# One core, sparse attention followed by a max-out layer: the written-out order of all tasks, the engines of the copies and the buffers exchanged for another set

## The chip, the cores and the metric

The kernel runs on one core of one Trainium2 chip. The metric is the device time of one execution in microseconds, lower is better. The core has a matrix engine (TensorE, PE in the profile, with its weight loads shown apart as PEld), VectorE (DVE), ScalarE (ACT), GpSimd (POOL), and SyncE (SP), which here only issues transfers. Each engine works through its own list of instructions in order and waits at semaphores for the others. Transfers run on 16 DMA engines beside them.

## The reference, cut to what matters

Four batches, eight heads, 768 positions, 64 values a head. Each query sees the 15 keys on either side of it and itself, and beside them 24 block keys: for every block of 32 keys their maximum, with the mean of the block's values.

```
k_sum = k.reshape(B, H, nb, 32, D).max(axis=3)
v_sum = v.reshape(B, H, nb, 32, D).mean(axis=3)
scores_l = scale * q @ k.T            # kept where |i - j| < 16
scores_s = scale * q @ k_sum.T + log(32)
a = softmax(concat(scores_l, scores_s))
x = (a @ concat(v, v_sum)).transpose(0, 2, 1, 3).reshape(3072, 512)
out = maximum(x @ w1, x @ w2) @ w_out     # w1, w2: 512 x 1024; w_out: 1024 x 512
```

Inputs and output are float32; the kernel computes in bfloat16 with float32 sums.

## The kernel before, in words

**Tasks.** The kernel first describes its whole work as 780 tasks (`op`, from line 140 of the listing on). A task is a small piece for one engine: one load, one cast of a loaded tile, three transposes, the score matrices of four windows, one exponential, one quarter of a hidden layer. It names the buffers it reads and writes. A buffer belongs to a `Ring`, a small set of slots of one tile shape (13 `land` tiles for loads, 8 PSUM banks, 4 `kqb`, 2 `vx`, 10 output tiles `o`, of which six lie in tiles that held w1 before, shown as `w1t` and `w1b`). A slot is given to the next buffer when the earlier one's last reader is done, and if a task is placed earlier than that, its engine waits.

**What sets the order.** `Plan.run` can find an order by replaying the tasks with assumed durations, but this kernel does not run it. It carries the outcome as three tables: `CFG["order"]`, the numbers of the tasks in the order in which they are issued; `CFG["engines"]`, a letter a task, which tells of a task that can run on several engines the one that it gets (T PE, D DVE, A ACT, P POOL, S a transfer by SP); and `CFG["slots"]`, the slot that each new buffer takes. `given` (line 225) emits the tasks by these tables:

```
    def given(self, order, slots):
        for t in order:
            for b in self.tasks[t].new:
                if b.slot is None:
                    b.take(slots.pop(0))
            self.tasks[t].fn(self.tasks[t].letter)
```

Since every engine keeps to its list, the tables fix what stands behind what on each engine and in SP's queue of transfers.

**Stages.** Batch 0 comes first: `prep` casts k and q (L596 and L598 are the copy helper: casts, placements, copies), turns them by TensorE (L629, into PSUM) and places them; the block maxima are L655. `spread_v` prepares v: copies shifted by half a window into `vx`, block means by TensorE (L523, L569) and their copies into `vx` (from `apart` in batch 0, from `sums` later). `scores` is L706 (its mask in batch 0 is a matmul, L695, later a product on DVE, L730), the exponential is L720 on ACT, `values` L762 and L767, the division L818 and L821 on DVE into `xs`. `xs` is turned into `xt`, by TensorE in batch 0 (L836 and a copy) and by a DMA transpose from SP in the later batches (L827). Some of k and q of batches 2 and 3 are also turned by DMA transposes (L633). Early in the kernel, TensorE has nothing real to do for stretches, and 14 pairs of matmuls on the identity (L990, `warm`) stand there.

**Weights.** `load_w12` loads w1 and w2 in four quarters of two pieces each (L857). `wd n` (L865) is the difference w2 - w1 of quarter n in bfloat16: one instruction on DVE or four on POOL. The max-out is computed as relu(x (w2 - w1)) and x w1, the latter folded into w1 w_out (`w1o`, L905). `maxout` multiplies by `wd` (L921, "hidden", eight matmuls of 256 columns; hidden quarters 1 and 3 in the task names need wd 1 and wd 3, the others wd 0 and wd 2), takes the relu (L930 on ACT, L932 on DVE), and `out_part` adds x w1o (L948) and g w_out (L955), copies the bank to an `o` tile (L598) and stores it (L966, L968) from SP's or ACT's queue.

A task name such as "hidden 023" means batch 0, group of positions 2, quarter 3; "scores 321" batch 3, heads 4 to 7, group 1; "copy out 121" batch 1, group 2, half 1.

## Time and profile before

| | |
|---|---|
| median of 3 runs | 165.75 us (164.71 to 165.79) |
| the profiled execution's own time | 165.96 us |
| its span, first to last instruction | 164.2 us |
| TensorE busy | 153.8 us, 94% of the span |
| weight loads, DVE, ACT, POOL busy | 100.0, 112.1, 92.9, 63.6 us |
| matmuls | 1812 |
| read from and written to HBM | 25.17 MB, 6.29 MB |

An execution's time is its span and some 1.8 us around it. Busy times are unions, so pipelined instructions are not counted twice. The clock that was granted to TensorE is 1.00 in every stretch.

### The profile page before, as it was taken

Reading aid. Unit: us, or ns where it says so; the run is one execution under the profiler, and the core shown is the slowest. Engines: PE = TensorE matmul, PEld = TensorE weight load, DVE = VectorE, ACT = ScalarE, POOL = GpSimd, SP = SyncE. Lnnn points to the kernel's source line nnn. Section 1 sums busy time; section 2 is a strip of 40 time slices with the busy share of each in tenths; the row PEclk is TensorE's granted clock in tenths of the full one; section 3 lists DMA queues with packets and bytes.
Section 4 is the critical chain, followed back from the end, with each engine's and each line's share of the span. In section 5 each row is a group of like instructions: output and inputs, shape, how many; then the busy total and the mean of one; then the engine's idle time right before and its main releaser. Section 6 shows DMA issues by size and latency. Waiting matters only on the chain.

```text
span 164.2 us, 4482 instructions
## 1 busy us (share of the span) xinstructions
PE 153.8 (94%) x1812; PEld 100.0 (61%) x1812; DVE 112.1 (68%) x224; ACT 92.9 (57%) x134; POOL 63.6 (39%) x123
## 2 busy tenths in 40 slices
PE   5789977999999999999999999999899999999992
PEld 2346656998465554676687646778545467766651
DVE  3697797579866799977979974759756655063221
ACT  3469986694677698938796645382927312012010
POOL 6059949403343389654673654034730000000000
PEclk9999999999999999999999999999999999999999
DMA  4999999999999899997989996897999987111015
GB/s 155 288 326 309 254 364 371 395 379 381 288 191 271 176 290 258 157 260 131 205 187 241 226 151 106 208 268 144 239 230 360 305 156 187 36 64 70 0 67 188
DMA packets 67700, 36.46 MB, mean 222 GB/s; under 512 B 54624, under 2 KB 61664, under 8 KB 67680
## 3 DMA queue, kind: packets, MB, share of 16 engines
q1 hardware_dynamic: 66208, 33.76, 86.1%
q10 hardware_dynamic: 1472, 2.43, 4.4%
q8 instruction: 14, 0.23, 0.6%
q14 instruction: 6, 0.05, 0.1%
HBM read 25.17 MB, written 6.29 MB: 192 GB/s over the span
## 4 chain that ended last, share of the span: by engine, by line
PE 74%; DVE 9%; DMA 8%; SPq 2%; issue 2%; ACT 2%; ACTq 0%; DVEq 0%
PE banks L955 22%; PE banks L921 19%; PE banks L948 11%; DMA out_dram<-o 6%; PE banks L905 4%; PE banks L629 4%; PE banks L762 4%; PE banks L706 3%; DMA land<-in_k_dram 2%; PE banks L990 2%; DVE vx L598 2%; SPq L827 2%; DVE ks L655 2%; DVE kx L598 1%; DVE xs L821 1%
## 5 line engine op out<-in xcount | busy, mean ns | idle before, releaser
L955 PE MATMUL banks<-wo,g 128*128 128x512 bf16 (+2 forms) x208 | 46.5, 363 | 0.0
L921 PE MATMUL banks<-xt,wd 128*128 128x256 bf16 x384 | 45.5, 273 | 0.0
L921 PEld LDWEIGHTS <-wd 128*128 128x128 bf16 x384 | 37.3, 98 | 7.3
L955 PEld LDWEIGHTS <-g 128*128 128x128 bf16 x208 | 18.7, 98 | 17.3
L720 ACT ACTIVATE pb<-banks 128x1024 bf16<-128x1024 f32 x24 | 23.6, 1026 | 7.8 <-PE banks L706 5.4
L948 PE MATMUL banks<-w1o,xt 128*128 128x512 bf16 (+2 forms) x104 | 23.7, 363 | 0.3 <-DVE o L598 0.3
L932 DVE TENSOR_SCALAR g<-banks 128x512 bf16<-128x512 f32 x21 | 14.1, 685 | 8.7 <-PE banks L921 8.5
L930 ACT ACTIVATE g<-banks 128x512 bf16<-128x512 f32 x27 | 15.2, 603 | 8.1 <-PE banks L921 8.0
L598 POOL COPY vx<-sums 32x792 bf16<-32x792 bf16 x15 | 14.8, 988 | 12.6 <-ACT sums L598 7.1
L730 DVE TENSOR_TENSOR pb<-pb,mask 128x1024 bf16<-128x1024 bf16 (+1 forms) x24 | 16.1, 697 | 4.2 <-ACT pb L720 3.8
L821 DVE TENSOR_TENSOR xs<-banks,inv 128x512 bf16<-128x512 f32 x24 | 16.0, 687 | 3.6 <-DMA xt<-xs 3.0
L598 ACT COPY o<-banks 128x512 f32<-128x512 f32 (+1 forms) x8 | 4.4, 545 | 24.8 <-PE banks L955 23.7
L596 POOL CAST kqb<-land 128x256 bf16<-128x256 f32 (+1 forms) x22 | 10.9, 528 | 18.7 <-DMA land<-in_q_dram 9.8
L948 PEld LDWEIGHTS <-xt 128*128 128x128 bf16 x104 | 9.9, 98 | 9.7 <-issue 0.5
L655 DVE TENSOR_REDUCE ks<-kx 128x24 bf16<-128x768 bf16 x16 | 15.0, 944 | 0.2
L596 POOL CAST vx<-land 128x384 bf16<-128x384 f32 x20 | 10.6, 554 | 8.3 <-DMA land<-in_v_dram 8.3
L598 DVE COPY o<-banks 128x512 f32<-128x512 f32 (+2 forms) x10 | 6.2, 620 | 10.9 <-PE banks L955 8.8
L598 DVE CAST kqb<-land 128x768 bf16<-128x768 f32 x12 | 7.2, 612 | 6.7 <-DMA land<-in_k_dram 2.7
L629 PE MATMUL banks<-ident,kqb 128*128 128x128 f32 x60 | 9.6, 277 | 1.7 <-DVE kqb L598 1.7
L598 ACT CAST kqb<-land 128x768 bf16<-128x768 f32 x11 | 10.4, 944 | 1.2 <-DMA land<-in_k_dram 1.1
L762 PEld LDWEIGHTS <-pb 128*64 128x64 bf16 (+1 forms) x384 | 7.9, 110 | 4.7 <-issue 2.6
L762 PE MATMUL banks<-vx,pb 128*64 128x65 bf16 (+1 forms) x384 | 9.4, 196 | 1.2 <-DVE xs L821 0.6
(88 smaller groups left out, 183.4 us busy)
## 6 DMA issues: line engine op xcount, KB each, us to landing
land<-in_k_dram SPq DMA_DIRECT2D x16, 384.0 KB, 5.4
land<-in_v_dram SPq DMA_DIRECT2D x16, 384.0 KB, 6.8
land<-in_q_dram SPq DMA_DIRECT2D x16, 384.0 KB, 5.9
land<-in_moe_w_dram SPq DMA_DIRECT2D x8, 512.0 KB, 9.5
land<-in_moe_w_out_dram SPq DMA_DIRECT2D x4, 512.0 KB, 9.9
out_dram<-o SPq DMA_DIRECT2D x7, 256.0 KB, 2.3
out_dram<-o ACTq DMA_DIRECT2D x4, 256.0 KB, 3.2
out_dram<-w1t SPq DMA_DIRECT2D x3, 256.0 KB, 4.0
```

The costliest lines, as they stand in the source:

```text
L596: nc.gpsimd.tensor_copy(out=o[:, at:at + step], in_=i[:, at:at + step])
L598: {"D": nc.vector.tensor_copy, "A": nc.scalar.copy, "P": nc.gpsimd.tensor_copy}[e](out=o, in_=i)
L629: nc.tensor.transpose(out=bank(ps)[:, 128 * j:128 * j + 128], in_=src.ap[:].bitcast(F32)[:, 128 * j:128 * j + 128], identity=ident32[:])
L655: op("D", 0.95, lambda e: nc.vector.tensor_reduce(out=ks.ap[:, 0:nb], in_=free(kt(), 128, [256, NM], [192, 2], [32, 2], [1, 32]), axis=AX. ...
L720: op("A", {"A": 1.03}, lambda e: nc.scalar.activation(out=spread(pb.ap[:, 0, 0:1], [192, 8], [128, 2], [1, 64]) if PW > 128 else spread(pb ...
L730: nc.vector.tensor_tensor(out=o, in0=o, in1=spread(mask[:, 2 * u:2 * u + 1, 0:1], [0, n], [64, 2], [1, 64]), op=ALU.mult)
L762: nc.tensor.matmul(out=o, lhsT=p[r], rhs=vx[b].ap[r, par, hp + n, 2 * grp + u, a, 0:D + 1], start=(PW == 128 or par == 0), stop=(last and ...
L821: op("D", 0.69, lambda e: nc.vector.tensor_tensor(out=x.ap[:].rearrange("p n u a d -> p n (u a) d"), in0=spread(bank_tile[:, ps.ap, 0:1], ...
L921: nc.tensor.matmul(out=bank(ps)[:, 256 * s:256 * s + 256], lhsT=wd_tile[:, quarter, c, 128 * s:128 * s + 128], rhs=x.ap[:, c, :], start=(c ...
L930: nc.scalar.activation(out=o, in_=bank(ps), func=ACT.Relu)
L948: nc.tensor.matmul(out=bank(ps, c1 - c0), lhsT=x.ap[:, c, sl], rhs=w1o[c].ap[:, cols], start=(c == 0), stop=False)
L955: nc.tensor.matmul(out=bank(ps, c1 - c0), lhsT=g.ap[:, f, sl], rhs=wo[f // 2].ap[:, f % 2, cols], start=False, stop=(f == FC - 1))
```

## The change

The three tables are replaced; the tasks, their functions, their shapes and their dependencies stay as they are. 181 of the 780 tasks get another engine; the order is another one on every engine, and so are the slots. The DVE has 210 tasks before and after, ACT 143 before and 155 after, POOL 82 and 68, SP 106 and 108, TensorE 239 both times. The new tables were found by a replay in which VectorE may get in between the parts into which a GpSimd copy or difference is cut.

```
 CFG["order"] = list(map(int, """
-44 32 2 0 3 10 12 1 4 6 11 15 13 8 112 20 30 26 56 25 46 113 116 9 122 7 123 126 14 47 16 117 34 118 132 168 28 23 133
...
+4 32 3 26 30 31 19 112 113 27 1 0 2 44 116 10 12 15 16 46 56 132 122 9 117 123 25 133 34 6 118 11 13 33 126 14 128 119
...
 CFG["engines"] = "".join("""
-PDPPPDDDPAPDPDDDDPTTTTTTTTTTTTTTSSSAAAATDDPPSSSADPATAAPPSSSPDDPTADDDSSSPDDPTADDPSSDPTASSPATDSSDATDSSPATASDSASASDDTDTAD
...
+PPPDDDPDPAPPDPDDDPTTTTTTTTTTTTTTSSSAAAATADDDSSSPPDDTDADPSSSPPPPTADPPSSSDDDPTADDDSSDATASSPATASSPATASSPDTDSPSASDSPATATDD
...
 CFG["slots"] = list(map(int, """
-0 1 0 0 0 0 0 0 0 0 0 0 1 0 2 1 3 0 0 0 1 1 1 0 0 0 0 0 4 0 0 2 4 0 0 0 1 5 2 0 0 0 0 0 2 0 0 1 4 1 0 1 4 1 0 0 0 0 0
...
+0 0 1 0 1 0 0 1 1 0 0 0 0 0 2 3 0 1 0 0 0 1 0 0 4 0 0 0 0 5 1 0 0 0 0 1 0 0 2 4 2 0 0 0 0 0 1 0 0 1 0 2 1 0 1 6 7 2 0
...
```

Three places of the resulting lists follow. First DVE's list at the start of the kernel, where the first k tiles are prepared. `kqb` is a cast k or q tile, `kx` a placed one, `ks` its block maxima; `hide`, `amean`, `apart` are constants that are filled once. Before:

```order
L368 MEMSET apart_99 128x264
L390 COPY hide<-hide 64x64
L412 MEMSET amean 128x384
L393 COPY hide<-hide 128x128
L598 CAST kqb_75<-land_63 128x2x3x2x64
L598 CAST kqb_76<-land_62 128x2x3x2x64
L362 MEMSET apart_98 32x8x2
L362 MEMSET apart_99 32x8x2
L396 MEMSET hide 64x16
L397 MEMSET hide 32x48
L402 MEMSET amean 32x6x2 x4
L655 TENSOR_REDUCE ks_100<-kx_79 128x24
```

After:

```order
L337 MEMSET vx_95 128x96x2
L337 MEMSET vx_94 128x96x2
L598 COPY kx_79<-banks 128x6x2x64
L390 COPY hide<-hide 64x64
L412 MEMSET amean 128x384
L402 MEMSET amean 32x6x2 x4
L598 CAST kqb_75<-land_65 128x2x3x2x64
L655 TENSOR_REDUCE ks_100<-kx_79 128x24
L598 COPY kx_79<-kx_79 128x32
L396 MEMSET hide 64x16
L397 MEMSET hide 32x48
L598 COPY kx_79<-ks_100 128x6x2x32
```

The casts of the first two k tiles have gone to ACT, DVE places the first one, and the fillings of `hide` and `amean`, which stood ahead of anything loaded, now stand behind that placement.

Second, POOL's list around the differences of the weights (`wd`). Before:

```order
L596 CAST vx_94<-land_69 128x6x64 x2
L598 COPY vx_94<-vx_94 32x2x64
L596 CAST vx_94<-land_70 128x6x64 x2
L598 COPY vx_94<-vx_94 32x2x64
L598 COPY vx_94<-apart_99 32x528
L865 TENSOR_TENSOR wd<-land_62,land_65 128x256 x4
L865 TENSOR_TENSOR wd<-land_64,land_63 128x256 x4
L596 CAST w1b_124<-land_68 128x512 x2
```

After:

```order
L598 COPY vx_94<-vx_94 64x12x64
L598 COPY vx_94<-vx_94 32x2x64
L598 COPY vx_94<-apart_99 32x528
L598 COPY vx_94<-apart_98 32x528
L865 TENSOR_TENSOR wd<-land_62,land_64 128x256 x4
L865 TENSOR_TENSOR wd<-land_66,land_63 128x256 x4
L865 TENSOR_TENSOR wd<-land_69,land_68 128x256 x4
L596 CAST wo_130<-land_65 128x512 x2
```

The first two differences (wd 3 and wd 1) stay here; a third (wd 2), which DVE made before, is now behind them, and DVE keeps wd 0 alone. In SP's list the two pieces of wd 3 and of wd 1 are the 13th to 16th load in both kernels, behind twelve loads of q, k and v of batch 0; behind them come one k tile and then, after the change, the two pieces for wd 2 and the two for wd 0, where before a k tile stood among these four and the two of a pair were apart.

Third, SP's queue at the first store of the output (`out_dram<-o`, batch 0, group 0, half 0, "store 000") among the transposes of batch 2 (`xt`) and of k and q of batch 3 (`kt`). Before:

```order
L827 DMA_TRANSPOSE xt_113<-xs_110 128x4x128
L633 DMA_TRANSPOSE kt_104<-kqb_75 128x6x128
L428 DMA land_62<-in_k_dram 128x2x384
L827 DMA_TRANSPOSE xt_114<-xs_111 128x4x128
L827 DMA_TRANSPOSE xt_114<-xs_112 128x4x128
L428 DMA land_63<-in_q_dram 128x12x64
L966 DMA out_dram<-o_126 128x512
L827 DMA_TRANSPOSE xt_115<-xs_110 128x4x128
```

After:

```order
L428 DMA land_62<-in_q_dram 128x12x64
L470 DMA land_67<-in_v_dram 128x12x64
L966 DMA out_dram<-o_127 128x512
L827 DMA_TRANSPOSE xt_113<-xs_109 128x4x128
L633 DMA_TRANSPOSE kt_103<-kqb_75 128x6x128
L827 DMA_TRANSPOSE xt_113<-xs_110 128x4x128
L633 DMA_TRANSPOSE kt_104<-kqb_77 128x6x128
L827 DMA_TRANSPOSE xt_114<-xs_111 128x4x128
```

The store stands ahead of all transposes of batch 2, eight transfers earlier. In both kernels the copy "copy out 121" takes the `o` tile that this store empties. The second copy of that kind, "copy out 211", takes the tile that "store 011" empties; that store was the third of a run of three (111, 101, 011) and is the second now (111, 011).

## What the change will do to the time

> **What bounds the kernel now.** I read the page first, then the busy time of five stretches, because shares over the whole span mix stages that are limited by different things. The busy times of the page:
>
> ```profile
> PE 153.8 (94%) x1812; PEld 100.0 (61%) x1812; DVE 112.1 (68%) x224; ACT 92.9 (57%) x134; POOL 63.6 (39%) x123
> ```
>
> The view by stretches gives, for each, its length and then busy time and instructions of PE, PEld, DVE, ACT and POOL, the granted clock, and the DMA share:
>
> ```profile
> 0.00:29.34 29.34, 23.47 (x363) 14.91 (x364) 22.10 (x64) 19.66 (x27) 19.04 (x46) 1.00 1.03 297
> 29.34:100.00 70.66, 70.66 (x879) 46.57 (x876) 56.62 (x102) 51.05 (x72) 35.24 (x63) 1.00 1.09 242
> 100.00:130.00 30.00, 28.76 (x327) 18.35 (x316) 20.64 (x39) 17.48 (x27) 9.33 (x14) 1.00 0.97 236
> ...
> 160.96:164.20 3.24, 0.00 (x0) 0.00 (x0) 0.29 (x1) 0.04 (x1) 0.00 (x0) 1.00 0.50 164
> ```
>
> The matrix engine is the bound: from 29.34 to 100 it is never idle, and its 1812 matmuls stay the same ones. So the span is 153.8 plus its idle time, and the idle time stands in three places: 5.87 us before the first hidden layer (29.34 - 23.47), 1.24 us between 100 and 130, and 3.24 us behind the last matmul, where the last copy and store run; the stretch left out has next to none. An order of tasks can gain only there, some 7 us at the utmost, and can lose anywhere. The profiled execution took 165.96 us, 1.76 beside its span of 164.20. It lies 0.21 us above the median of the runs shown, 165.75; the sum below starts from 165.96.
>
> **First stage, what the first hidden layer waits for.** Timeline rows of TensorE, POOL and DVE (start, duration; in brackets the idle time ahead and what ended it):
>
> ```profile
> 29.01 0.50 PE L629 MATMUL banks<-ident,kqb 128*128 128x128 f32 x3
> 29.34 2.78 PE L921 MATMUL banks<-xt,wd 128*128 128x256 bf16 x24
> ...
> 23.35 5.53 POOL L865 TENSOR_TENSOR wd<-land,land 128x256 bf16<-128x256 f32 x8 [0.30 <-DMA land<-in_moe_w_dram]
> ...
> 5.19 1.07 DVE L598 CAST kqb<-land 128x768 bf16<-128x768 f32 x2 [1.99 <-DMA land<-in_k_dram]
> ...
> 27.26 0.75 DVE L598 COPY xt<-banks 128x512 bf16<-128x512 bf16 x2
> ```
>
> The hidden layer needs wd 3 and wd 1, which POOL finishes at 28.88, and xt of group 2, whose last copy DVE finishes at about 27.6. POOL could not begin earlier: it waited 0.30 us for the weights to land. In the new lists the same twelve loads of q, k and v and the same four pieces of weights stand in front, so by the bytes ahead of them they land at the same time, and wd 1 ends at 28.9 again. Then three transposes and the first hidden layer, at 29.1 to 29.3.
>
> Does DVE keep up? I compare what stands in its list up to that xt copy, with durations from the groups by shape:
>
> ```profile
> L598 DVE CAST kqb<-land 128x768 bf16<-128x768 f32 x12 | 7.2, 612 | 6.7 <-DMA land<-in_k_dram 2.7 <-DMA kt<-kqb 2.0 <-DMA land<-in_q_dram 1.3
> L598 DVE COPY qx<-banks 128x768 bf16<-128x768 bf16 x8 | 4.4, 550 | 1.1 <-PE banks L629 1.1
> L821 DVE TENSOR_TENSOR xs<-banks,inv 128x512 bf16<-128x512 f32 x24 | 16.0, 687 | 3.6 <-DMA xt<-xs 3.0 <-DVE inv L818 0.2
> L598 DVE COPY vx<-apart 32x528 bf16<-32x528 bf16 x3 | 1.2, 432 | 0.1
> L598 DVE COPY xt<-banks 128x512 bf16<-128x512 bf16 x5 | 1.8, 417 | 1.0 <-PE banks L836 1.0
> L598 DVE CAST wo<-land 128x1024 bf16<-128x1024 f32 x2 | 1.4, 688 | 0.2 <-DMA land<-in_moe_w_out_dram 0.2
> ```
>
> Casts of k and q go from five to four (-0.61), placements from six to five (-0.55), divisions ahead of that copy from six to five (-0.69), shifts of v from five to four (about -0.5; they are copies like the two of 0.39 and 0.25 shown under the rivals, and three large ones go for two small ones). Copies from `apart` go from three to five (+0.86), and there come one cast of v (+0.6, priced as a cast of k), one cast of a w1 piece, as large as one of w_out (+0.69), one more `ks` copy (+0.25), one more xt copy (+0.42), and a copy of 32 columns (+0.1). Net **+0.6**. The fillings that moved from idle time to behind the first placement:
>
> ```profile
> 2.37 0.18 DVE L390 COPY hide<-hide 64x64 bf16<-64x64 bf16 x1 [0.21 <-POOL hide L378]
> 2.69 0.38 DVE L412 MEMSET amean<- 128x384 uint32 x1
> 12.36 1.24 POOL L596 CAST kqb<-land 128x256 bf16<-128x256 f32 x3 [1.38 <-DMA land<-in_k_dram]
> 12.77 0.59 DVE L598 CAST apart<-banks 64x128 bf16<-64x128 f32 x2 [0.46 <-PE banks L523]
> 19.90 0.28 DVE L598 CAST apart<-banks 64x128 bf16<-64x128 f32 x1 [0.61 <-ACT apart L598]
> ```
>
> They add **+0.6** (0.18 and 0.38). DVE also starts later. It began at 5.19, with the second load; the seventh was there at 12.36, so a load takes about 1.4 us (7.17 over 5), and the first lands between 3.8 and 5.19. ACT now casts it (0.94, row below), three transposes take 0.5, so the placement begins between 5.3 and 6.6; I take 5.6, **+0.4**. In sum DVE is done 1.6 us later than 27.6, at 29.2, if it waits as long as before. Its waits between its first cast and that copy were five, 1.6 us together (the first and the longest are the last two rows above); without any it would be done at 27.6. POOL's 28.9 lies between the two, so DVE has lost most of the 1.3 us that it was ahead. I take 29.1 for the first hidden layer: -0.2. One turn of xs (4 transposes, 0.2) moves from ahead of it to behind it and takes half of that back: **-0.1**, between -1.4 and +2.
>
> ACT gets more of this stage: two k casts of 0.94 and more before its first exponential, which stood at 16.73.
>
> ```profile
> L598 ACT CAST kqb<-land 128x768 bf16<-128x768 f32 x11 | 10.4, 944 | 1.2 <-DMA land<-in_k_dram 1.1
> 16.73 2.86 ACT L720 ACTIVATE pb<-banks 128x1024 bf16<-128x1024 f32 x3 [0.17 <-PE banks L706]
> 6.49 0.80 ACT L598 COPY kx<-banks 128x768 bf16<-128x768 bf16 x1 [4.46 <-PE banks L629]
> ```
>
> ACT idled 4.46 us until 6.49, and the two casts fill that idle time, so I cost them at nothing; where the first load is late they cost up to 0.9.
>
> **wd 0 and wd 2.** Casts of single pieces show when the 18th and 19th load were there, and one group row prices a wd on DVE:
>
> ```profile
> 29.40 1.05 ACT L598 CAST w1b<-land 128x1024 bf16<-128x1024 f32 x1 [1.55 <-DMA land<-in_moe_w_dram]
> 30.73 1.17 POOL L596 CAST w1b<-land 128x512 bf16<-128x512 f32 x2 [1.86 <-DMA land<-in_moe_w_dram]
> L865 DVE TENSOR_TENSOR wd<-land,land 128x1024 bf16<-128x1024 f32 x2 | 2.4, 1224 | 1.9 <-DMA land<-in_moe_w_dram 1.9
> ```
>
> wd 2 goes from DVE, where it took 1.22, to POOL, third in a row at 2.76 (half of 5.53). The 18th and 19th load are now its pieces: POOL works from 30.7 to 33.5. The pieces of wd 0 follow at 1.33 each, 33.4, and DVE ends at 34.6. TensorE meanwhile has six hidden quarters that need only wd 1 and wd 3 (0.9 each, a third of the 2.78 for 24 matmuls) and 0.7 of turns: 29.1 + 5.4 + 0.7 = 35.2. The margin is 0.6 us; if DVE's relus ahead of wd 0 delay it, TensorE stands, up to 1 us. I take **+0.1**. Behind POOL's longer block wait two casts of w_out and block copies of k of batch 1. TensorE comes to them only behind another six hidden quarters, 5.4 us, which hide them; a POOL that is later than that costs its excess.
>
> **The idle time after 100.** The chain that ended last leaves TensorE here for two stores, and three TensorE rows carry the stalls:
>
> ```profile
> 104.62 4.71 DMA out_dram<-o
> ...
> 117.47 5.08 DMA out_dram<-o
> 110.17 1.02 PE L948 MATMUL banks<-w1o,xt 128*128 128x512 bf16 x4 [0.33 <-DVE o L598]
> 116.33 0.41 PE L706 MATMUL banks<-kt,kx 64*128 64x64 bf16 x16 [0.45 <-ACT g L930]
> ...
> 123.27 0.42 PE L706 MATMUL banks<-kt,kx 64*128 64x64 bf16 x19 [0.46 <-ACT o L598]
> 92.77 2.01 SPq L827 DMA_TRANSPOSE xt<-xs  x1
> ```
>
> 0.33, 0.45 and 0.46 make the 1.24. The first: copy out 121 needs the `o` tile of store 000, issued only at 104.62 and landed 4.7 us later; until then a bank is held. In the new queue that store stands ahead of the first transpose of batch 2, which went out at 92.77, so it lands some ten microseconds before it is needed. The third: copy out 211 waits likewise for store 011, which is now second, not third; each of the three stores has about 1.7 us of the 5.08, more than the 0.46. The second comes from ACT, where three relus stand together; one of them is on DVE now. I take the 1.24 as gone but for 0.1: **-1.1**. At worst all of it stays.
>
> **What is late next.** From the view of the transfers, the transposes of xs by SP and their median time from issue to landing:
>
> ```profile
> xt<-xs SPq DMA_TRANSPOSE x18, 3.7
> ```
>
> In batch 3 values 301 is now followed by five output pieces (0.9 each; the four matmuls of the first row of stalls take 1.02 with their drain) and two values tasks, about 5 us, until a hidden layer needs its transpose; division and transpose take 0.69 + 3.7 = 4.4. A margin of some 0.6; I take **+0.2**, between 0 and 1. The tail keeps its form: 0, give or take 0.3.
>
> Sum: 165.96 - 0.1 + 0.1 - 1.1 + 0.2 = **165.0** rounded, against 165.75.
>
> **Rivals.** *Slower: DVE becomes the bound of the first stage, because it and GpSimd hold each other up.* That they do is in the trace: the same DVE copy takes 0.39 and 0.25, and POOL's copies from `apart` 0.80 each in one place (three in 2.41) and 0.62 in another.
>
> ```profile
> 14.00 0.39 DVE L598 COPY kx<-ks 128x384 bf16<-128x384 bf16 x1
> 17.95 0.25 DVE L598 COPY kx<-ks 128x384 bf16<-128x384 bf16 x1
> 13.66 2.41 POOL L598 COPY vx<-apart 32x528 bf16<-32x528 bf16 x3
> 16.40 0.62 POOL L598 COPY vx<-apart 32x528 bf16<-32x528 bf16 x1
> ```
>
> DVE has some 22 copies and casts there that read SBUF. At 0.14 each that is 3.1 us on 29.1, and the first hidden layer moves to 32.2: 165.0 + 3.1 = 168.1. It decides as soon as DVE is later than POOL's 28.9, and at three quarters of that price it passes 167.4, 1% above the median (1% is about what a measurement of this kernel tells from no change). For it: no slack is left. Against it: the before kernel has most of these delays in its durations already. [...] Chance 0.23.
>
> *Faster than forecast: the weights land earlier.* The four pieces were issued between 13.76 and 17.9, waiting for `land` tiles, which the new lists free earlier.
>
> ```profile
> 13.76 4.10 SPq L857 DMA_DIRECT2D land<-in_moe_w_dram  x4
> GB/s 155 288 326 309 254 364 371 395 379 381 288 191 271 176 290 258 157 260 131 205 187 241 226 151 106 208 268 144 239 230 360 305 156 187 36 64 70 0 67 188
> ```
>
> If they landed 2 us earlier, DVE's best case of 27.6 would decide, the first hidden layer would begin at 27.8, and the time would be 163.7 (165.0 - 1.3). Against it: the DMA engines were moving 250 to 370 GB/s all that while, so there was a backlog and no hole. Chance 0.20.
>
> *No difference: the stalls change places.* The orders move what TensorE does not wait for, and margins of 0.6 turn into stalls of about a microsecond: 165.9. Chance 0.14.
>
> **How the numbers follow.** Forecast 0.43, slower 0.23, faster 0.20, no difference 0.14. Faster by over 1% means below 164.1: the third case and a little of the forecast, 0.24. Slower by over 1% means above 167.4: 0.24. Within 1%: 0.52. The range leaves out a tenth on each side: 163.5, just below the fast rival, to 168.2, which takes in the slow one at its price; the forecast's own range is 164.2 to 166.0.
>
> **What would show it.** Right: TensorE busy 153.8 again, first L921 at about 29.1, the rows of wd on POOL three in a row from 23.3, TensorE without a wait for an `o` copy after 100. Wrong: the first L921 later than 30 with DVE's xt copies ahead of it; stalls of TensorE between 30 and 50 that end with wd 0 or a relu; waits for xt before the last hidden layers; or busy time of TensorE that is not 153.8.

## The result, and the profile after

The changed kernel takes 171.23 us (median of 4, 170.34 to 173.66) where the kernel before took 165.23 in the same comparison: 1.033 of its time, 95% interval 1.026 to 1.040. It is slower, and outside the range of the prediction. The profiled execution took 170.34 us. Ratios here and below leave out executions that were over 1.5% longer than the fastest of their kernel; the profile of first_after_rest_before is of one that was.

The page of the changed kernel, busy times and granted clock:

```profile
span 168.6 us, 4486 instructions
...
PE 156.4 (93%) x1812; PEld 100.7 (60%) x1812; DVE 111.6 (66%) x223; ACT 102.9 (61%) x148; POOL 57.4 (34%) x103
...
PEclk9959999999999999999999999999999999999999
```

The view by stretches, cut at its own first hidden layer and last matmul, and two stretches of 4 us near the start (length, then busy time and instructions of PE, PEld, DVE, ACT, POOL, then the granted clock, DMA share, GB/s):

```profile
0.00:32.90 32.90, 25.69 (x359) 15.56 (x360) 23.98 (x62) 21.75 (x31) 19.46 (x45) 0.95 1.02 307
32.90:100.00 67.10, 66.62 (x810) 44.33 (x808) 54.56 (x99) 51.83 (x76) 29.20 (x45) 1.00 1.01 233
100.00:130.00 30.00, 30.00 (x363) 19.31 (x361) 22.14 (x42) 20.18 (x29) 8.76 (x15) 1.00 0.93 202
130.00:165.58 35.58, 34.09 (x286) 21.49 (x284) 10.53 (x21) 9.09 (x16) 0.00 (x0) 1.00 0.43 119
165.58:168.60 3.02, 0.00 (x0) 0.00 (x0) 0.35 (x2) 0.00 (x0) 0.00 (x0) 1.00 0.44 138
...
8.00:12.00 4.00, 2.85 (x9) 1.41 (x10) 3.40 (x8) 1.56 (x2) 1.87 (x4) 0.64 1.11 334
12.00:16.00 4.00, 4.00 (x31) 2.55 (x30) 2.56 (x7) 2.62 (x7) 1.78 (x4) 0.93 1.19 307
```

Timeline rows of TensorE, POOL, DVE:

```profile
9.15 0.90 PE L629 MATMUL banks<-ident,kqb 128*128 128x128 f32 x3 [1.85 <-DVE kqb L598]
32.23 0.27 PE L877 MATMUL banks<-identity,w1b 128*128 128x128 bf16 x2 [0.16 <-issue]
32.90 1.91 PE L921 MATMUL banks<-xt,wd 128*128 128x256 bf16 x16
139.32 1.92 PE L921 MATMUL banks<-xt,wd 128*128 128x256 bf16 x16 [1.48 <-DMA xt<-xs]
...
13.10 0.83 POOL L598 COPY vx<-vx 64x768 bf16<-64x768 bf16 x1
20.75 1.81 POOL L598 COPY vx<-vx 32x128 bf16<-32x128 bf16 x3
24.38 1.33 POOL L598 COPY vx<-apart 32x528 bf16<-32x528 bf16 x2
25.79 9.14 POOL L865 TENSOR_TENSOR wd<-land,land 128x256 bf16<-128x256 f32 x12
...
13.29 1.11 DVE L598 CAST kqb<-land 128x768 bf16<-128x768 f32 x1
21.88 0.80 DVE L598 COPY kx<-kx 128x384 bf16<-128x384 bf16 x1
25.18 0.71 DVE L598 COPY vx<-vx 32x640 bf16<-32x640 bf16 x1
26.71 1.46 DVE L598 COPY vx<-apart 32x528 bf16<-32x528 bf16 x2
```

The span is 4.4 us longer than before. The first hidden layer starts at 32.90 where it was 29.34: **+3.56**. Between it and the last matmul TensorE's idle time is 1.97 us (0.48 + 1.49) where it was 1.24: **+0.73**, and its busy time 130.71 (66.62 + 30.00 + 34.09) where it was 130.35 (70.66 + 28.76 + 30.93, the last being the rest of its 153.82): **+0.36**. The stretch behind the last matmul is 3.02 for 3.24: **-0.22**. Of the 3.56, 2.22 are busy time of TensorE (25.69 for 23.47) and 1.34 idle time. So two places matter: everything ahead of 32.90, and the wait of 1.48 us for an xt at 139. The idle time between 100 and 130 is gone.

Four things in the first stage differ from before. TensorE's granted clock falls to 0.64 behind an idle time of 1.85 us. DVE copies that stand beside POOL's copies are long: the cast of a k tile 1.11 where the others take 0.59 to 0.60, and the last row's two copies 1.46 together, of a form that takes 0.29 where it stands alone. GpSimd begins the differences of the weights at 25.79, not at 23.35, and did not wait for their pieces. And so wd 1, which the first hidden layer needs too, is ready at 32.19 (GpSimd's eighth piece, 31.46 + 0.73) where it was 28.88: VectorE's last copy of xt ahead of that layer, which ends at 32.3, and wd 1 are late together.

### The profile page after: what moved, and what is told of

Its sections match the earlier page's. It is cut to its first block, busy times and chain, and to the rows that moved or that the text cites. A ratio compares the mean times of both kernels' runs of the same rounds, so it can differ in the third digit from the quotient of the medians.

```text
span 168.6 us, 4486 instructions
## 1 busy us (share of the span) xinstructions
PE 156.4 (93%) x1812; PEld 100.7 (60%) x1812; DVE 111.6 (66%) x223; ACT 102.9 (61%) x148; POOL 57.4 (34%) x103
## 4 chain that ended last, share of the span: by engine, by line
PE 65%; DVE 15%; DMA 9%; issue 4%; ACT 4%; SPq 1%; DVEq 0%
PE banks L921 19%; PE banks L955 18%; PE banks L948 10%; PE banks L905 4%; DMA land<-in_k_dram 4%; DMA xt<-xs 3%; DVE vx L598 3%; PE banks L629 2%; PE banks L762 2%; DVE kx L598 2%; PE banks L990 2%; PE banks L706 2%; DVE kqb L598 2%; DMA kt<-kqb 2%; DVE xs L821 2%
## 5 line engine op out<-in xcount | busy, mean ns | idle before, releaser
L921 PE MATMUL banks<-xt,wd 128*128 128x256 bf16 x384 | 46.0, 273 | 1.6 <-DMA xt<-xs 1.5
L955 PE MATMUL banks<-wo,g 128*128 128x512 bf16 (+2 forms) x208 | 47.3, 363 | 0.0
L921 PEld LDWEIGHTS <-wd 128*128 128x128 bf16 x384 | 37.3, 98 | 9.9 <-DMA xt<-xs 2.0
L598 POOL COPY kx<-kx 128x32 bf16<-128x32 bf16 (+1 forms) x12 | 5.1, 426 | 33.3 <-DVE kx L598 23.6
L598 ACT COPY o<-banks 128x512 f32<-128x512 f32 (+1 forms) x10 | 5.6, 562 | 17.5 <-PE banks L955 9.4
L730 DVE TENSOR_TENSOR pb<-pb,mask 128x1024 bf16<-128x1024 bf16 (+1 forms) x24 | 14.8, 639 | 1.8 <-ACT pb L720 1.7
L598 DVE CAST kqb<-land 128x768 bf16<-128x768 f32 x16 | 11.5, 723 | 4.7 <-DMA kt<-kqb 1.5
L598 DVE COPY o<-banks 128x512 f32<-128x512 f32 (+1 forms) x8 | 4.6, 588 | 12.5 <-PE banks L955 12.3
L598 POOL COPY vx<-sums 32x792 bf16<-32x792 bf16 x12 | 10.7, 889 | 3.7 <-ACT sums L598 3.1
L990 PE MATMUL banks<-identity 128*128 128x512 bf16 x28 | 10.0, 490 | 1.7 <-DVE identity L328 1.7
L629 PEld LDWEIGHTS banks<-ident,kqb 128*128 128x128 f32 x60 | 7.5, 148 | 5.3 <-DVE kqb L598 2.3
```

The source lines that it names most:

```text
L598: {"D": nc.vector.tensor_copy, "A": nc.scalar.copy, "P": nc.gpsimd.tensor_copy}[e](out=o, in_=i)
L629: nc.tensor.transpose(out=bank(ps)[:, 128 * j:128 * j + 128], in_=src.ap[:].bitcast(F32)[:, 128 * j:128 * j + 128], identity=ident32[:])
L730: nc.vector.tensor_tensor(out=o, in0=o, in1=spread(mask[:, 2 * u:2 * u + 1, 0:1], [0, n], [64, 2], [1, 64]), op=ALU.mult)
L921: nc.tensor.matmul(out=bank(ps)[:, 256 * s:256 * s + 256], lhsT=wd_tile[:, quarter, c, 128 * s:128 * s + 128], rhs=x.ap[:, c, :], start=(c ...
L955: nc.tensor.matmul(out=bank(ps, c1 - c0), lhsT=g.ap[:, f, sl], rhs=wo[f // 2].ap[:, f % 2, cols], start=False, stop=(f == FC - 1))
L990: nc.tensor.matmul(out=bank(ps), lhsT=identity[:], rhs=spread(identity[:, 0:1], [0, 4], [1, 128]), start=True, stop=True)
```

## The experiments

The theory from these views: the list of VectorE (DVE) is the bound of the first stage, since DVE and GpSimd hold each other up; and a transpose late in SP's queue costs the 1.48. Its rivals: the fall of TensorE's clock began the loss; the new lists of the rest lose by themselves; and, from the fourth group on, TensorE waits for its own instructions. The ratio is to the kernel before, run beside it on the same chip. In some of these kernels the line numbers are one to six higher than in the profiles above (L922 or L927 is L921).

| kernel | first hidden layer, us | ratio, 95% interval |
|---|---|---|
| the changed kernel | 32.90 | 1.033, 1.026 to 1.040 |
| after_warm_ahead | 31.73 | 1.032, 1.023 to 1.042 |
| after_late | 31.57 | 1.013, 1.009 to 1.018 |
| after_warm_late | 31.88 | 1.015, 1.006 to 1.024 |
| after_act_sums | 31.45 | 1.015, 1.008 to 1.023 |
| after_late_fewer | 31.41 | 1.021, 1.016 to 1.026 |
| pool_small_2 | 32.27 | 1.014, 1.005 to 1.023 |
| pool_small_fewer | 30.48 | 1.022, 1.017 to 1.027 |
| first_after_rest_before | 32.56 | 1.023, 1.016 to 1.030 |
| first_before_rest_after | 29.55 | 1.034, 1.024 to 1.045 |
| first_before_late | 29.31 | 1.024, 1.017 to 1.031 |
| before_gap | 33.21 | 1.025, 1.014 to 1.037 |
| before_gap_small | 32.84 | 1.010, 1.003 to 1.018 |
| before_stores, and again | 29.03, 29.07 | 0.996, 0.991 to 1.001; 1.004, 1.000 to 1.008 |
| before_fewer | 28.18 | 1.000, 0.996 to 1.004 |
| stores_fewer | 29.70 | 1.004, 1.001 to 1.008 |

### Is it the clock?

after_warm_ahead, TensorE's list in the changed kernel:

```
 turn k01
 warm
+warm
+warm
+warm
 turn k02
-warm
-warm
 hide 001
-warm
 sums 00
```

> The changed kernel; three of TensorE's warm pairs, which stood behind turn k02, stand ahead of it, nothing else moves. In the changed kernel TensorE idles 1.85 us ahead of turn k02, and its granted clock is 0.64 in the next 4 us and 0.93 in the 4 after. If that fall of the clock began the loss, the idle time is about 0.6 us here, the granted clock stays at 1.00, TensorE's busy time goes from 156.4 back to about 153.8, turn q00 starts at 13 or earlier where it was 15.3, the first hidden layer comes at 30 to 31 where it was 32.9, and the time is 168 to 169. If VectorE and GpSimd holding each other up are the whole cause (the slower rival of the prediction), the clock and the busy time come back as well, but the first hidden layer stays at 32.3 or later and the time at 170 to 171. If the new lists of ACT and GpSimd are the cause (wrap k03 on GpSimd behind place k03 on ACT), GpSimd's idle time of 4.7 us up to 18.6 shrinks only as far as turn k03 comes earlier, and the time lies between.

before_gap, TensorE's list in the kernel before:

```
 turn k01
-hide 001
-warm
-warm
 turn k02
+hide 001
+warm
+warm
 warm
```

> The kernel before; the two warm pairs and the mask matmuls that stood ahead of turn k02 stand behind it, so that TensorE idles about 1.9 us there where it idled 0.7 us. If an idle time of that size lets the clock fall by itself, the granted clock is 0.6 to 0.7 in the slice behind it, TensorE's busy time is 155 to 157 where it was 153.8, the first hidden layer moves from 29.3 to 30 or 31, and the time is 166 to 167.5. If the clock stays at 1.00, the time is the one before, 165.2, and the fall in the changed kernel has another cause.

before_gap_small moves the two warm pairs only; hide 001 stays where it was.

> The kernel before; only two warm pairs, not the mask matmuls, stand behind turn k02, so that TensorE idles 1.5 to 1.6 us ahead of it. If before_gap lost its 3 us to the fall of the clock, and that needs an idle time of more than 1.6 us, the granted clock stays at 1.00, the first hidden layer comes at most 0.9 us later (two pairs more in the queue, at 0.43 each), at 29.4 to 30.2, and the time is 165.3 to 166.2. If the longer queue behind turn k02 was what lost, the first hidden layer comes at 31.5 or later and the time is 167 or more. A fall of the clock here would show that 1.5 us are enough.

By stretches, after_warm_ahead:

```profile
8.00:12.00 4.00, 2.84 (x19) 1.43 (x18) 3.32 (x8) 1.55 (x3) 2.00 (x5) 1.00 1.12 328
```

before_gap, stretches and one row of its timeline:

```profile
8.00:12.00 4.00, 2.78 (x11) 1.37 (x12) 3.94 (x9) 1.96 (x4) 2.15 (x5) 0.79 1.13 321
12.00:16.00 4.00, 4.00 (x25) 1.97 (x24) 0.58 (x2) 1.56 (x4) 1.24 (x3) 0.79 1.15 319
...
9.22 0.52 PE L630 MATMUL banks<-ident,kqb 128*128 128x128 f32 x3 [2.02 <-DVE kqb L599]
```

In before_gap the clock falls behind one idle time of 2.02 us: the mean is 0.79 in both stretches of 4 us, TensorE is busy without a break from 12 to 16, and DVE works 0.58 of those 4 us. The kernel takes 1.025 of its time. With an idle time of 1.53 (before_gap_small) the clock stays at 1.00 and the ratio is 1.010. That the difference of 1.5% is the price of the fall is not shown: the two also differ by the place of hide 001, their intervals overlap, their first hidden layers lie 0.37 us apart, and of the two profiled executions that of before_gap_small was the longer (169.05 us against 168.31). Within one kernel, single executions with a mean clock of 0.99 took from nothing to some 2 us more (first_before_late 168.91 among 168.81 to 169.23, after_warm_late 169.84 against 167.57 to 168.16). That before_gap_small lost anything was not expected; the reason is in the fourth group.

In the changed kernel the repair brings the clock back and the first hidden layer from 32.90 to 31.73. That is a third of the 3.56 and lies between what the two theories expected. TensorE's busy time went from 156.4 to 155.3 only, not to the 153.8 that both had: most of its rise is not the clock, and the runs do not show what it is. The time hardly moves: the wait for xt at 139 grows from 1.48 to 1.91. **The clock is a part of the loss in the first stage, and not the largest.**

### Which half of the lists?

The tasks up to the first hidden layer (177 are common to both kernels) come from one kernel, all others from the other; where a slot is still held at the seam, the next free one is taken.

```
 order, engines, slots:
-  up to hidden 023 as in the changed kernel, then as in the changed kernel
+  up to hidden 023 as in the kernel before, then as in the changed kernel   (first_before_rest_after)
+  up to hidden 023 as in the changed kernel, then as in the kernel before   (first_after_rest_before)
```

> All tasks up to the first hidden layer in the order, on the engines and in the slots of the kernel before; the rest as in the changed kernel. If the loss arises ahead of the first hidden layer, that comes at 29.3 again and the time is 166.3 to 167: the 170.3 of the changed kernel's profile less 3.6, with the wait for xt 301 of about 1.5 us still ahead of hidden 310. If the rest of the new lists loses by itself, 168 or more. If the wait for xt 301 came only from the delay of the first stage, 165 to 165.5.

> The other half: all tasks up to the first hidden layer as in the changed kernel, the rest as in the kernel before. If the loss arises ahead of the first hidden layer, that comes at 32.9 and the time is 168.5 to 169.5 (165.2 and 3.6), with the idle time of 1.2 us between 100 and 130 back and no wait of 1.5 us for xt before hidden 310. If the rest of the new lists is the cause, about 166.

TensorE's waits in first_before_rest_after:

```profile
31.12 3.65 PE L922 MATMUL banks<-xt,wd 128*128 128x256 bf16 x32 [0.54 <-ACT xt L599]
37.46 2.47 PE L922 MATMUL banks<-xt,wd 128*128 128x256 bf16 x21 [1.04 <-POOL wd L866]
```

Both halves lose, 1.023 and 1.034, and together more than the change itself. With the first stage of before the hidden layers start at 29.55, but then TensorE waits 0.54 for an xt, 1.04 for wd, 0.9 in three waits between 63 and 88, and 1.07 for xt 301. The new lists of the rest did not use the early start. In the changed kernel, with its late first stage, TensorE's only waits of this size behind 33 are 0.39 us at 92 and the 1.48. The seam makes some loads late, so I read no more from these two than that.

### VectorE beside GpSimd

In pool_small seven of GpSimd's copies shrink, so that batch 0's values come from incomplete data; all of VectorE's tasks stay.

```
             o, i = aps(e) if by_engine else aps()
+            if e == "P" and label in SMALL:
+                o, i = o[:, 0:1], i[:, 0:1]
```

> The kernel of after_warm_ahead; seven copies into vx on GpSimd (odd v020, v040, v041, v042, all sums 021, 040, 041) copy only the first element of their second axis, so that batch 0's values are computed from incomplete data (vx is filled with ones at the start for that, on VectorE, in its idle time). VectorE's own list is unchanged. In after_warm_ahead VectorE works without a wait from the cast of k03 at 13.4 to the last xt copy at 31.0, and five of its instructions that run beside these copies take 1.09, 0.62, 0.43, 0.79 and 0.71 us. If GpSimd's copies stretch them, they take about 0.59, 0.29, 0.29, 0.25 and 0.32 here, 1.9 us less together, and the first hidden layer comes at about 29.8 where it was 31.7; the two copies all sums 060 and 061, beside the differences of the weights, stay at 0.71. If the lengths belong to the instructions themselves (their tile, their partitions), they stay, and the first hidden layer at 31.7.

Filling vx cost VectorE 5.4 us, the start became late (first hidden layer at 33.18), and the stage says nothing. The durations do. The slice left the three copies from apart whole, since their second axis has one element; only odd v020 and odd v04x became short. The cast of k03 went to 0.60, all sums 000 to 0.29 and tails k03 to 0.26, while all sums 001 (0.62) and odd v061 (0.71), which stand beside those copies from apart, stayed as they were. pool_small_2, on the kernel of after_warm_late (last group), shrinks these too and fills less:

```
+                o, i = (o[:, :, 0:1], i[:, :, 0:1]) if label.startswith("all") else (o[:, 0:1], i[:, 0:1])
```

> The kernel of after_warm_late; seven copies into vx on GpSimd (odd v020, v040, v041, v042, all sums 021, 040, 041) copy only a small first part, so that batch 0's values are computed from incomplete data. In pool_small the filling of vx took 5.4 us of VectorE and made the whole start late; here it is a quarter of that or less and lies in VectorE's idle time before 6 us. If GpSimd's copies hold VectorE's up, the cast of k03, all sums 001, all sums 000, tails k03 and odd v061 take 0.59, 0.29, 0.29, 0.25 and 0.32 us where they took 1.09, 0.62, 0.43, 0.79 and 0.71; VectorE, which had no idle time from 13.4 to the last xt copy, is done 1.9 us earlier, at 29.1, the first hidden layer comes at 29.9 where it was 31.9 (GpSimd's own work, shorter too, lets wd 1 end at about 29.7), and the time is 1.5 to 2 us less, 166 to 166.5. If something else is the bound behind VectorE (TensorE's queue, the weights), the instructions are shorter but the first hidden layer stays at 31 or later.

Its DVE rows, to be read against the last four of the changed kernel, and its two waits of TensorE:

```profile
13.42 0.61 DVE L603 CAST kqb<-land 128x768 bf16<-128x768 f32 x1
20.21 0.26 DVE L603 COPY kx<-kx 128x384 bf16<-128x384 bf16 x1
22.96 0.31 DVE L603 COPY vx<-vx 32x640 bf16<-32x640 bf16 x1
24.10 1.45 DVE L603 COPY vx<-apart 32x528 bf16<-32x528 bf16 x2
...
25.40 0.24 PE L711 MATMUL banks<-qx,kx 64*128 64x64 bf16 x6 [0.70 <-issue]
31.61 0.27 PE L882 MATMUL banks<-identity,w1b 128*128 128x128 bf16 x2 [2.06 <-issue]
```

All five durations came as expected, and the two copies beside the differences of the weights kept their length, 1.45 for two. **GpSimd stretches these copies of VectorE, by 0.14 to 0.55 us each.** In the changed kernel the cast of k03 looks like a wait for the end of GpSimd's piece: it starts 0.19 into a GpSimd copy of 0.83 and ends 0.47 behind it, which is most of its own 0.60. Not all of VectorE's instructions are stretched: there a block maximum (TENSOR_REDUCE) takes 0.95 from 12.29 on, beside GpSimd's work, and 0.94 from 8.98 on, while GpSimd idles.

VectorE's last xt copy ended at 29.76 (30.84 in after_warm_late). But the first hidden layer came at 32.27, no earlier: TensorE stood still twice with nothing to wait for in the profile. The other way to relieve VectorE:

```
 VectorE:  odd v061, sums 061, w1b 3, -all sums 060, -all sums 061, inv 002
 ScalarE:  sums 060, +all sums 060, +all sums 061, exp 020
```

> The kernel of after_warm_late; the two copies all sums 060 and 061 go from VectorE, where they take 0.71 us each beside GpSimd's differences of the weights, to ACT, ahead of exp 020, in ACT's idle time. All work is done. If VectorE is the bound, its last xt copy ends 1.4 us earlier, at 29.6, and the first hidden layer is then set by wd 1 on GpSimd, which ended at 30.7 and is held up a little less: 30.5 to 30.9 where it was 31.9, and the time 0.8 to 1.3 us less, 166.7 to 167.2. If the delay of exp 020 by two copies of 0.64 on ACT is passed on, the first hidden layer stays at 31.5 or later.

It came out as the second case, but for 0.05 us: the first hidden layer came at 31.45, as exp 020, now behind two copies, ended at 27.12, and VectorE stood 1.97 us for the values made from it. What the copies had saved was lost to that wait but for 0.4 us.

### What TensorE waited for: its instructions

The rows "issue" say that TensorE waited for nothing that the profile shows. Counting matmuls up to them by the view of stretches, for the kernel before (two rows), the changed kernel, and pool_small_2 (two):

```profile
0.00:22.29 22.29, 18.07 (x223) 10.24 (x223) 16.22 (x49) 15.31 (x23) 12.76 (x37) 1.00 1.02 271
0.00:28.50 28.50, 22.63 (x351) 14.07 (x352) 21.75 (x62) 19.66 (x27) 18.66 (x46) 1.00 1.03 295
```

```profile
0.00:32.23 32.23, 25.03 (x350) 14.91 (x351) 23.31 (x61) 21.08 (x29) 18.79 (x44) 0.95 1.01 305
```

```profile
0.00:25.39 25.39, 19.70 (x222) 10.90 (x223) 18.11 (x50) 17.55 (x25) 11.30 (x38) 1.00 1.00 278
0.00:31.61 31.61, 23.77 (x350) 14.34 (x351) 22.77 (x62) 21.91 (x30) 16.09 (x44) 1.00 1.01 300
```

The order of the work differs, the tasks there differ, but the waits stand at matmul 222 or 223 and 350 or 351: 128 matmuls apart, with as many weight loads. And the transfers have a queue named instruction. In the kernel before a window from 26.0 to 26.3 holds the start of one of its packets (at 26.19), in pool_small_2 one from 29.2 to 29.3 (at 29.24):

```profile
q8 instruction: 1, 0.02, 21.8%
```

```profile
q8 instruction: 1, 0.02, 69.3%
```

The packet takes 1.05 and 1.11 us (its share of 16 engines in that window), so it is there at 27.2 and 30.35, and TensorE goes on at 28.50 and 31.61, 1.3 us later in both. The test is to shift the count: 15 matmuls of the warm pairs left out.

```
-            for _ in range(2):
+            for _ in range(FEWER.get(n, 2)):
                 nc.tensor.matmul(out=bank(ps), lhsT=identity[:], ...
```

> The kernel of pool_small_2 (batch 0's values from incomplete data), and 15 of the 28 matmuls of the warm pairs are left out (the computation needs none of them); the four pairs at the start stay. In pool_small_2 VectorE was done at 29.8, but TensorE waited 0.70 us ahead of its matmul 222 and 2.06 us ahead of its matmul 350, counted from 0, for nothing that the profile names, and the first hidden layer came at 32.3. In all kernels of this study such waits stand at these two numbers, 128 matmuls or 256 instructions with their weight loads apart, and end about 1.3 us behind a packet of 16 KB in the queue named instruction. If TensorE waits there for its instructions, the second of these places lies 15 matmuls later in the work, in the first hidden layer, which begins as soon as VectorE's xt and the turns are done: 30.0 to 30.6, and the time is 1.5 to 2 us less than pool_small_2, 166.5 to 167.2. If the waits belong to the tasks at which they stood (the turns), the first hidden layer stays at 32.

> The kernel of after_warm_late, all work done, with the same 15 warm matmuls left out. There VectorE was done at 30.8 and TensorE waited 0.58 us ahead of matmul 350. By the theory of the instructions only these 0.6 us go: first hidden layer at 31.2 to 31.4 where it was 31.9, since VectorE is the bound here, and the time 0.4 to 0.7 us less, 167.3 to 167.6. If TensorE's queue (the warm pairs themselves) held the stage up, 30.5 or earlier.

> The kernel before with 15 of the 28 warm matmuls left out. There TensorE waited 0.53 us ahead of matmul 223 and 1.04 us ahead of matmul 351 with no cause named; the first hidden layer begins at matmul 363, by now 348. If instructions were awaited, there is no wait of this kind ahead of the first hidden layer but perhaps one in it, and it comes at 28.9 to 29.1 where it was 29.3, set by wd 1 on GpSimd (28.9); the time is 0.2 to 0.5 us less. If the clock falls because fewer matmuls fill the stage (the idle times become up to 1.4 us), TensorE's busy time rises and the time is 166.5 or more.

> The kernel of before_stores with the same 15 warm matmuls left out: the sum of both edits, 0.2 to 0.9 us less than the kernel before if both terms hold; 165.5 or more if neither can be told from no change.

pool_small_fewer, timeline, and the count at its second wait:

```profile
30.48 0.82 PE L927 MATMUL banks<-xt,wd 128*128 128x256 bf16 x6
32.64 1.03 PE L927 MATMUL banks<-xt,wd 128*128 128x256 bf16 x8 [1.33 <-issue]
...
0.00:32.63 32.63, 24.22 (x350) 15.07 (x351) 23.12 (x63) 22.03 (x30) 17.58 (x46) 0.95 1.02 303
```

before_fewer, timeline:

```profile
28.70 1.53 PE L922 MATMUL banks<-xt,wd 128*128 128x256 bf16 x11 [0.24 <-POOL wd L866]
```

The wait kept its number, 350, and moved into the hidden layer, 15 matmuls later in the work. **These waits go by the count of TensorE's instructions, not by the work:** 128 matmuls and as many weight loads, 256 instructions, lie between the two. Since a packet of the queue named instruction had come 1.3 us ahead of the end of the wait in the two cases above, I read them as waits of TensorE for its instructions; no view names that cause. The first hidden layer came at 30.48, as expected: VectorE's xt was ready at 30.19 (29.78 + 0.41) and wd 1 at 30.11, and TensorE had worked without a break since 28.00, when a division of VectorE had ended, so that VectorE's list decides by this division. But 1.33 us were then lost in the layer, and the time did not fall. after_late_fewer has the same matmuls left out and differs from pool_small_fewer in GpSimd's copies alone: 31.41 and 1.021 against 30.48 and 1.022. GpSimd's shorter copies are thus worth 0.93 us of the first stage there, though pool_small_fewer's clock fell for a while (0.76 and 0.81, last section), and no time that can be told. Where TensorE had to wait at these numbers, it stood between 0.16 us (the changed kernel) and 2.35 us (before_gap_small); the DMA share up to the waits is 1.00 to 1.03 in the rows above.

This explains before_gap_small: it had two such waits, 1.78 (which the profile puts down to a copy of w1b) and 2.35, where the kernel before had 0.53 and 1.04. And it corrects what bounded the kernel before: matmul 351 started at 28.50, and the first hidden layer 0.84 behind it, at 29.34, not because of wd 1. Without the wait it starts at 28.2 and then stands 0.24 for wd (before_fewer). Its measured time is the same nonetheless, 1.000. That the time did not follow the first hidden layer, and why after_late_fewer is not faster than the kernel that it comes from, stays open. In the profile of stores_fewer one reason can be seen: TensorE stood 1.34 us, up to 29.31, for the cast of a k tile on ScalarE, which had waited 2.19 us for its load.

### The late transpose

after_late, SP's queue in the changed kernel; after_warm_late has this on top of after_warm_ahead, first_before_late on top of first_before_rest_after:

```
 store 101
-store 010
-store 120
-store 020
 store 211
-store 021
 xt 320
 xt 321
 xt 301
+store 010
+store 120
+store 020
+store 021
```

> The kernel of after_warm_ahead, and in SP's queue the stores 010, 120, 020 and 021, whose tiles were ready long before, stand behind xt 301 where they stood ahead of xt 320. If these stores made the transposes of batch 3 late, xt 320, 321 and 301 are issued 1 to 2 us earlier, the wait ahead of hidden 310 (1.9 us there) goes to 0.5 or less, and the time is 1.4 to 1.9 us less than that of after_warm_ahead, 168.1 to 168.7. If the transposes themselves set the pace (they landed 2.4 us apart in the changed kernel), the wait falls by no more than 0.5.

> The changed kernel, and of the repairs only the one of SP's queue: the stores 010, 120, 020 and 021 stand behind xt 301. The changed kernel takes 1.033 of the time before, after_warm_ahead (three warm pairs earlier) 1.032, after_warm_late (both edits) 1.015. If the wait for xt 301 is a cost of its own, 1.48 us in the changed kernel, it goes to 0.3 or less here, the first hidden layer stays at 32.9, and the ratio is 1.023 to 1.026. If the late first stage already covers it (the transposes then have more time), the ratio stays at 1.03; if the first stage's delay by the clock costs nothing once this wait is gone, it is 1.015 as in after_warm_late.

> The kernel of first_before_rest_after (the first stage of the kernel before, the rest of the changed one), and the stores 010, 120, 020 and 021 stand behind xt 301 in SP's queue. There the first hidden layer came at 29.6, but TensorE waited 0.54 and 1.04 us for xt and wd between 31 and 38, 0.9 us in three waits between 63 and 88, and 1.07 us for xt 301, and the ratio was 1.034. If the rest of the new lists can use the earlier start once xt 301 is in time, the ratio is 1.012 to 1.02 (the wait of 1.07 gone, 0.6%, and as much again as the same edit brought in after_warm_late beyond its wait). If the lost time only moves to other waits on transfers, 1.027 or more.

The changed kernel: a store and the three transposes in SP's issues, and a row of the chain that ended last:

```profile
127.34 0.45 SPq L966 DMA_DIRECT2D out_dram<-w1t  x1
130.52 4.96 SPq L827 DMA_TRANSPOSE xt<-xs  x3
...
134.10 5.18 DMA xt<-xs
```

after_warm_late, the same:

```profile
127.44 6.63 SPq L827 DMA_TRANSPOSE xt<-xs  x3
...
132.88 4.05 DMA xt<-xs
```

In the changed kernel six stores stand ahead of the three transposes, four of them of tiles that were ready long before. With those four behind, the transposes go out from 127.44 on, that of xt 301 takes 4.05 where it took 5.18, the wait falls from 1.91 (after_warm_ahead) to 0.35, and the ratio from 1.032 to 1.015; the spans of the profiled executions differ by 1.3 us (167.7 and 166.4). after_late alone has 1.013, with 0.69 us of the wait left; there the idle time ahead of turn k02 was 1.60 and the clock did not fall (the mean clock is 0.997 to 1.000 in all six executions, and 0.98 to 0.99 in all four of the changed kernel), so it is no clean fourth of the four combinations and doesn't tell whether the two costs add. What it says with the other: with most of the wait for the transpose gone, and with the clock at 1.00, the change costs 1.3 to 1.5%, 2.2 to 2.5 us, as much as the first hidden layer is late by (31.57 and 31.88 against 29.34: 2.2 and 2.5). That the one is the cause of the other is not shown, since no version with the new lists whose hidden layers began earlier was faster. first_before_late stands at 1.024 where it was 1.034 without the edit, with intervals that overlap, though its hidden layers start at 29.31: the rest of the new lists gives the early start back by waits of 0.3 to 0.7 us for xt, wd, kx and o between 31 and 92, and of 0.88 for xt 301.

### The stores

before_stores does in the kernel before what the prediction counted as the change's gain.

```
 SP:   +store 000, xt 200, xt 220, xt 221, xt 201, -store 000
 SP:   +store 011, store 111, store 101, -store 011
 ACT:  +relu 221, wrap k30, all sums 301, -relu 221
```

> The kernel before with three moves that answer its idle time after 100: store 000 ahead of the first transpose of batch 2, store 011 ahead of store 111 in SP's queue, and relu 221 ahead of two copies in ACT's list. By the prediction's term for this place the three waits of TensorE (0.33, 0.45, 0.46) go but for 0.1 and the time falls by 1.1, to 164.4 or less. If the waits change places (the last transposes and their hidden layers then come too early for their data), it stays at 165.5.

> The kernel of before_stores once more, in more rounds, to tell whether it beats the kernel before: 0.3 to 0.7% less if the term for the stores is real (0.9959 there, with 1 still in the interval), 1.000 if it was chance.

By stretches, before_stores:

```profile
29.03:130.00 100.97, 100.95 (x1203) 65.77 (x1201) 79.62 (x142) 68.70 (x99) 43.20 (x77) 1.00 1.06 243
```

The three waits are gone, and TensorE is busy for all but 0.02 us of 101. In the profile of the second comparison, of the same kernel, 1.25 us of idle time are back between 100 and 130, in other places:

```profile
100.00:130.00 30.00, 28.75 (x339) 18.49 (x326) 21.89 (x40) 18.14 (x27) 10.66 (x14) 1.00 0.96 222
...
107.20 3.65 PE L921 MATMUL banks<-xt,wd 128*128 128x256 bf16 x32 [0.72 <-DMA xt<-xs]
```

The other two are 0.22 and 0.30, near 123, for copies on ScalarE. So such waits change from one execution to the next, and one profile does not price them. The first comparison gave 0.996, the second 1.004: no gain that can be told. No version in this study beats the kernel before.

## Why the prediction was wrong

**What bounds the kernel.** Right that TensorE's idle time decides and that an order can lose anywhere. Not right that its busy time is a constant: it was 156.4, not 153.8, and 155.3 in after_warm_ahead with the clock at 1.00, so the fall of the clock is some 1 us of that (156.4 - 155.3). And the first stage of the kernel before ended with the wait of 1.04 us marked "issue", which stood in the trace of before and of which the prediction did not speak; wd 1 on GpSimd, which it named, was the next bound, half a microsecond earlier. The terms of the prediction's sum give 165.06, which it put as 165.0.

**First stage, -0.1.** This step failed: +3.56. I put DVE's end at 29.2 and let POOL's 28.9 decide. DVE ended at about 32.3 (31.87 + 0.42). What the runs showed in place of it: some 1.0 to 1.3 us go with the clock (first hidden layer at 31.6 to 31.9 in after_warm_ahead, after_late and after_warm_late, where it stayed up; 32.56 in first_after_rest_before). The rest is for the most part DVE's list. In after_warm_ahead it has one idle time, of 0.41 us, from the cast of k03 at 13.4 on, and from 10 us on eight copies stand in it so that GpSimd stretches them, by about 3.0 us together (each duration less that of the same form standing alone). I summed durations from before, where two such copies were stretched. With five of the eight stretches taken away DVE ended at 29.8, half a microsecond off my 29.2, so the count of work was about right and its price beside the other engine wrong. That DVE's list sets the first hidden layer is shown down to 30.5 (pool_small_fewer); in pool_small_2, with the same copies short, the wait of 2.06 us marked "issue" held it at 32.27.

POOL's part fell with it. Not the landing of the weights limited wd 3, which began at 25.79: two copies from `apart` stood ahead of it until 25.7, and these wait for sums that come through DVE, TensorE and ACT. wd 1 ended at 32.19, 0.1 us ahead of DVE's copy. And an earlier GpSimd would not have met the 28.9: in pool_small_2 it waited for the pieces of wd 1 until 27.28, and wd 1 ended at 30.07.

**wd 0 and wd 2, +0.1.** TensorE did not stand there in the changed kernel. The margin that I gave as 0.6 was there only because everything ahead was late: with the first stage of before TensorE waited 1.04 us for wd, the upper end of my range.

**The idle time after 100, -1.1.** In the profile the 1.24 us went, all of it. That this is worth 1.1 us of time could not be shown when it was done alone (0.996 and 1.004), and one of the two profiles of that has as much idle time there as the kernel before. So it is in part luck that the one profile of the changed kernel has none.

**What is late next, +0.2.** The right mechanism, mis-sized: 1.48. I set 0.69 for the division and 3.7, the median, for the transpose against 5 us of TensorE's work. Four rows of DVE and TensorE in the changed kernel:

```profile
131.97 0.70 PE L762 MATMUL banks<-vx,pb 128*64 128x65 bf16 x32
...
132.59 0.64 DVE L730 TENSOR_TENSOR pb<-pb,mask 128x1024 bf16<-128x1024 bf16 x1
133.14 0.20 DVE L818 RECIPROCAL inv<-banks 128x8 f32<-128x8 f32 x1
133.38 0.69 DVE L821 TENSOR_TENSOR xs<-banks,inv 128x512 bf16<-128x512 f32 x1
```

The values are there at 132.67 (131.97 + 0.70). A mask product stands ahead of the division, which ends at 134.07, so that 1.4 us pass in place of 0.69; and the transpose takes 5.18, with stores and two other transposes under way (4.05 in after_warm_late, with four of the stores behind it). A median hides just the case that matters.

**Rivals.** "DVE becomes the bound, as it and GpSimd hold each other up" named the main mechanism and came near in its place: 32.2 for the first hidden layer, measured 32.90, and 31.6 to 31.9 with the clock up. The size per copy was not 0.14 on 22 copies but 0.14 to 0.55 on eight; that both come to about 3 us is luck. It had a chance of 0.23, since I read "the kernel before has most of these delays in its durations already" as an argument against; the delays belong to the pairs of instructions that meet, and a new order makes new pairs. Its 168.1 lacked the late transpose. "The weights land earlier" did not show: GpSimd came to the pieces later than before and found them there. "The stalls change places" describes the end of the kernel, and before_stores, where the waits came back elsewhere in a second execution; not the size of the loss.

**What would show it** was answered: first L921 later than 30 with DVE's xt copies ahead of it, a wait for xt ahead of the last hidden layers, TensorE's busy time not 153.8. Of the four signs for wrong that I had listed only the stalls between 30 and 50 did not come.

## What to carry to other kernels

When an order is changed, price each copy of VectorE by what GpSimd will do at that moment, not by its duration in the old order: eight copies took 0.14 to 0.55 us more beside GpSimd here, about 3.0 us together. Count the matmuls up to the rows marked "issue": up to 33 us they stood at matmul 222 or 223 and 350 or 351 in every order that had them, with 0.16 to 2.35 us each. And ask of a stage that ends earlier whether each later stage, the last transposes above all, has its data early enough: with its hidden layers from 29.31 on, first_before_late still took 1.024 of the time.

## What the runs showed of the hardware that I had not expected

TensorE's clock fell early in the kernel behind a short idle time: behind 1.85 (the changed kernel), 2.02 (before_gap) and 2.22 us (pool_small) the mean granted clock was 0.64, 0.79 and 0.62 in the stretch from 8 to 12, while 1.53 (before_gap_small), 1.60 (after_late) and 1.62 (after_late_fewer) at that place left it at 1.00. The length of the gap does not decide by itself. In pool_small_fewer, with no gap above 1.44 but TensorE busy for only 1.74 us of the 4 from 8 to 12, the clock was 0.76 and 0.81 in the next two stretches; in before_fewer, with 1.71 of 4, it stayed up; and later gaps of 1.78 (after_act_sums), 2.06 (pool_small_2) and 2.35 (before_gap_small) left it up. Divided at the moments when the clock changes, the changed kernel shows the form, and after_warm_ahead an exception:

```profile
5.73:9.15 3.42, 1.57 (x9) 0.58 (x7) 2.04 (x9) 1.76 (x3) 0.50 (x2) 1.00 1.19 275
9.15:12.56 3.41, 3.41 (x10) 1.69 (x11) 3.18 (x10) 2.12 (x4) 2.34 (x6) 0.50 1.07 369
...
136.50:139.92 3.42, 1.51 (x14) 1.37 (x15) 1.66 (x3) 0.00 (x0) 0.00 (x0) 1.00 0.68 171
```

In all four traces with a fall the clock is at 0.50 for one stretch of 3.41 us, and in the 3.41 us ahead of it TensorE was busy for 1.25 to 1.74. When the nineteen traces are divided at this spacing from the first clock record of each (at 4.65 in the kernel before, 5.73 in the changed one, 7.41 at the latest), every other stretch up to the last matmul has 1.79 or more, but for one: 1.51 from 136.50 on in after_warm_ahead, behind which the clock stayed up. The gap of 2.35 thus lies across two stretches: within one it would have left no more than 1.06 of the 3.41 us for work. So sparse work counted too, not one gap alone. That the busy time of such a stretch decides is my reading of this division; the exception at 136.50 speaks against it as a rule, and what made it is not shown.

The waits marked "issue" up to 33 us stood 128 matmuls and as many weight loads apart, 256 instructions. In the nineteen profiles of this study the packet of the queue named instruction that came ahead of matmul 350 started 3.0 to 4.6 us behind matmul 222 (26.19 against 21.57 in the kernel before, 29.24 against 25.40 in pool_small_2), took 1.0 to 1.1 us, and TensorE, where it had to wait, went on 1.2 to 1.5 us later. An estimate from these times (3.0 + 1.0 + 1.2 to 4.6 + 1.1 + 1.5): 128 small matmuls with their weight loads take at least 5 to 7 us here, ahead of the first hidden layer, where the DMA share is 1.03 in the kernel before and 1.02 in the changed one; in the kernel before, 223 to 351 took 6.2.
